# Logits by column-group products, maximum in PSUM, attention weights turned on TensorE, and a listed order

## The chip, the cores and the metric

The kernel runs on one core of a Trainium2 chip. The metric is the device time of one launch in microseconds; it is given as the median of repeated runs. One further execution was taken by the hardware profiler, and all lines quoted below come from it.

## What is computed

A conditioned transformer block for 2048 tokens of width 512 in bf16: layer norm with a shift and scale computed from a condition vector, attention with 32 heads of 16 over a dilated window of eight earlier tokens (two apart), then a second layer norm and a gated feed-forward part of width 1792.

```python
def _A_ref(x, wqkv, wo):
    H = 32; Dh = D // H; W, dil = (8, 2)
    qkv = (lambda x, *d: x.transpose(*d))((x @ wqkv).reshape(B, S, 3, H, Dh), 2, 0, 3, 1, 4)
    idx = pos[:, None] - off[None, :]          # off = arange(W) * dil
    mask = idx >= 0
    ...
    logits = jnp.einsum('bhsd,bhswd->bhsw', q, kg) * scale
    logits = jnp.where(mask[None, None, :, :], logits, -1000000000.0)
    attn = _softmax(logits, axis=-1)
    o = jnp.einsum('bhsw,bhswd->bhsd', attn, vg)
    return (lambda x, *d: x.transpose(*d))(o, 0, 2, 1, 3).reshape(B, S, D) @ wo

def _B_ref(x, w1, w3, w2):
    return jnp.einsum('bsf,fd->bsd', _silu(x @ w1) * (x @ w3), w2)
...
h = _layernorm(x, axis=-1) * (1 + ca) + sa
x = x + ga * _A_ref(h, A_wqkv, A_wo)
h = _layernorm(x, axis=-1) * (1 + cb) + sb
x = x + gb * _B_ref(h, B_w1, B_w3, B_w2)
```

## The kernel before

The 2048 tokens are 16 tiles T of 128. All of x stays on chip, as do all weights. `_build` describes the work as operations: each names its engine, what it reads and writes, a cost in ns and a key for its priority. `Program.schedule` plays the operations through a model of the engines, always taking the ready one of least priority value, and so fixes the order of every engine's queue and the buffers; `synchronize` puts in the semaphore waits; `emit` writes five straight programs, one an engine. SP issues nearly all transfers, in its own fixed order, and a transfer that waits holds up those behind it.

The stages of a tile, which overlap freely across tiles:

- LN1 (`ln_stats`): `bn_stats` (L590) and `bn_aggr` on VectorE, two small steps on POOL (L596, L598), the normalisation on VectorE (L613). `ln_T` turns the tile on TensorE (L649) and ScalarE applies scale and shift on the way out (L657).
- q, k and v (`proj_qk`, `proj_v`; L702, L721), copied out of PSUM by ScalarE; v goes to a scratch in DRAM.
- Logits (`logits`): VectorE multiplies q with the eight shifted k (L752, 4096 elements a partition). TensorE sums each head's 16 products: for each of eight window places and four column blocks, the product block is loaded as weights and a 128x32 matrix of ones, `E_sb`, streams past (L761), 32 small products a tile. Tokens lie on partitions.
- Softmax: ScalarE takes the exponential out of PSUM (L775), without a maximum. VectorE masks tile 0 (L787), adds up in three steps (L791, L793, L795), takes the reciprocal (L797) and multiplies (L798).
- AV (`values`): the weights go to a scratch in DRAM and come back in another layout (two transfers a tile, pieces of 64 bytes on the way back); v comes back from its scratch in four transfers; VectorE multiplies (L821); TensorE sums with 32 small products (L830); ScalarE copies (L836); the output projection (L843) and the residual addition on VectorE (L847) follow.
- LN2: again `bn_stats`, POOL, a bias on VectorE (L603), and the normalisation on ScalarE (L609). From FFN group 3 on (`DMA_T[1]`) the turn is a DMA transpose (six tiles), before that TensorE's.
- Feed-forward: tiles in groups (`FFN`: 2, 4, 4, 4, 2). Each group has 14 units: products with w1 and w3 (L859), SiLU on ScalarE (L865), the multiplication on VectorE (L868). Then the products with w2 (L897; L885 for the last two tiles), the output addition (L907) and the store.

Before the first loads land TensorE runs products of ones (L551, 26 times four). The condition vector is turned by a product of four rows (L519) between them.

Of the kernel before, what the change touches and what calls it, by code (L numbers as in the profile page):

```python
# [22 lines left out]
NCH = S // 512  # L23
# [5 lines left out]
LAT = {"sp": 1900, "pe": 230, "dve": 70, "act": 150, "pool": 120}  # L29
DMA_RATE = 350  # L30
TABLE_LOAD = 1300
LOOK = 250


class Pool:
    def __init__(self, name, items):
        self.name = name
        self.free = [(0, i, item, []) for i, item in enumerate(items)]
        self.n = 0

    def take(self):
        return self.free.pop(0)

    def give(self, when, slot, item, ops):
        self.n += 1
        self.free.append((when, slot, item, ops))


class Val:


    def __init__(self, name, pool=None, at=None):
        self.name = name
        self.pool = pool
        self.at = at
        self.slot = None
        self.writers = []
        self.readers = []
        self.users = []
        self.left = 0  # L60
        self.sealed = False


class Op:
    __slots__ = ("eng", "fn", "cost", "pr", "deps", "vals", "n", "start", "end", "seen", "pos", "dma", "bytes",
                 "waits", "inc", "clock", "prev", "group", "table", "key", "follow", "led", "lock")

    def __init__(self, eng, fn, cost, key):
        self.eng, self.fn, self.cost, self.key = eng, fn, cost, key
        self.pr = 0  # L70
        self.table = None
        self.follow = None
        self.led = False
        self.deps = {}
        self.vals = []
        self.prev = []
        self.end = None
        self.dma = False
        self.lock = False
        self.bytes = 0  # L80
        self.inc = None
        self.group = [self]


class Program:
# [7 lines left out]
    def op(self, eng, fn, cost, key, r=(), w=(), part=(), after=(), dma=0, table=None, lead=None, lock=None, hold=()):  # L93
        o = Op(eng, fn, cost, key)
        o.lock = eng == "pool" and not dma if lock is None else lock
        o.table = table
        if lead is not None:
            lead.follow = o
            o.led = True
# [23 lines left out]
        if dma:  # L123
            o.dma = True
            o.bytes = dma
        return o

    def dma(self, out, in_, key, nbytes, r=(), w=(), part=(), after=(), eng="sp", cost=450, group=None, transpose=False):
# [8 lines left out]
        o = self.op(eng, fn, cost, key, r=r, w=w, part=part, after=after, dma=nbytes)  # L137
# [5 lines left out]
    def schedule(self, prio):  # L143


        ops = self.ops
        users = {o: [] for o in ops}
        missing = {}
# [874 lines left out]
```

## Time and profile before

| | |
|---|---|
| median of 3 runs | 251.25 us (251.13 to 251.63) |
| span of the profiled execution | 248.6 us |
| logits, one tile on TensorE (L761) | 32 products, 0.79 us in the chain |
| AV sum, one tile (L830) | 32 products, 0.79 us in the chain |
| multiplication for logits (L752) / AV (L821) | 2280 / 2283 ns, 16 each |
| `bn_stats` (L590) / `bn_aggr` (L591) | 678 / 182 ns, 32 each |
| halving additions L791, L793, L795 (a pair) | 420, 292, 225 ns |
| ScalarE normalisation (L609) | 805 ns, 16 times |
| DMA transpose | 6, issue 1.25 us, 2.4 us to landing |
| attention weights out / back | 2.1 / 2.4 us to landing, 16 each |

The profiled execution's span runs from the first to the last instruction; the runs' times hold the launch around it as well. A matmul's recorded duration runs from its start to its modelled end and overlaps the next one; the chain of waits shows what a run of them takes end to end. PE is TensorE, PEld its weight loads, DVE VectorE, ACT ScalarE.

### The profile page before, as it was taken

To read this page: it belongs to the slowest core of one execution; us is meant where nothing else is said; L and a number is where in the kernel's file an instruction comes from. 1 tells how busy PE (TensorE), PEld (TensorE's weight loads), DVE (VectorE), ACT (ScalarE), POOL (GpSimd) and SP (SyncE) were. 2 spreads that over 40 slices of the span, in tenths; PEclk is the share of its full clock that TensorE was granted. 3 is DMA by queue.
4 is the path that set the end of the run, shared out by engine and by line. 5 is a ranking of instruction groups with operands and counts; after the bars stand their busy time and mean duration, and the time that the engine had idled before them with its cause. 6 is when DMAs were issued, how large, how long until landed. Compare 5 with 4: busy or idle time off the path is not lost.

```text
span 248.6 us, 5772 instructions
## 1 busy us (share of the span) xinstructions
PE 243.5 (98%) x2437; PEld 149.2 (60%) x2437; DVE 186.8 (75%) x289; ACT 123.3 (50%) x216; POOL 21.3 (9%) x48
## 2 busy tenths in 40 slices
PE   8989999999999999999999999999999999999995
PEld 8857665475778856545665564455544444465784
DVE  3869799999898999999899897898942344232442
ACT  2369688864783466943230577443556333110320
POOL 3223500003200110000001101000110000000000
PEclk9999999999999999999999999999999999999999
DMA  6999969679979993336779270436032000001001
GB/s 221 356 327 274 279 201 299 140 199 286 314 223 259 319 288 100 63 54 157 200 232 263 56 229 22 85 46 169 3 84 63 4 0 0 21 24 42 21 3 42
DMA packets 49393, 37.09 MB, mean 149 GB/s; under 512 B 22216, under 2 KB 40664, under 8 KB 49368
## 3 DMA queue, kind: packets, MB, share of 16 engines
q1 hardware_dynamic: 49360, 36.73, 53.3%
q8 instruction: 19, 0.31, 0.5%
q14 instruction: 6, 0.05, 0.1%
q10 hardware_dynamic: 8, 0.00, 0.0%
HBM read 30.67 MB, written 5.26 MB: 145 GB/s over the span
## 4 chain that ended last, share of the span: by engine, by line
PE 94%; DMA 4%; SPq 1%; issue 0%; DVE 0%
PE pall L859 39%; PE pall L897 17%; PE pall L702 11%; PE pall L843 6%; PE pall L721 6%; PE pall L761 5%; PE pall L830 5%; DMA sb_wqkv<-in_A_wqkv_dram 4%; PE pall L885 2%; PE pall L649 2%; SPq L135 1%; PE pall L535 0%; PE pall L565 0%; PE pall L575 0%; DVE sb_o L907 0%
## 5 line engine op out<-in xcount | busy, mean ns | idle before, releaser
L859 PE MATMUL pall<-sb_h,sb_w 128*128 128x512 bf16 (+1 forms) x560 | 101.2, 336 | 0.0
L859 PEld LDWEIGHTS pall<-sb_h,sb_w 128*128 128x128 bf16 x560 | 53.8, 98 | 41.4
L865 ACT ACTIVATE sb_sg<-pall 128x512 bf16<-128x512 f32 (+1 forms) x70 | 35.3, 511 | 64.3 <-PE pall L859 64.3
L868 DVE TENSOR_TENSOR sb_hh<-sb_sg,pall 128x512 bf16<-128x512 bf16 (+1 forms) x70 | 39.0, 575 | 28.4 <-PE pall L859 28.4
L897 PE MATMUL pall<-sb_w,sb_hh 128*128 128x512 bf16 x196 | 44.4, 379 | 0.0
L752 DVE TENSOR_TENSOR sb_pq<-sb_q,sb_kT 128x4096 bf16<-128x4096 bf16 x16 | 36.1, 2280 | 0.5 <-ACT sb_kT L711 0.5
L702 PE MATMUL pall<-sb_h,sb_wqkv 128*128 128x512 bf16 (+1 forms) x160 | 31.0, 336 | 1.4 <-DMA sb_wqkv<-in_A_wqkv_dram 1.4
L897 PEld LDWEIGHTS pall<-sb_w,sb_hh 128*128 128x128 bf16 x196 | 18.9, 98 | 21.1
L821 DVE TENSOR_TENSOR sb_vsh<-sb_vsh,sb_al 128x4096 bf16<-128x4096 bf16 x12 | 27.2, 2283 | 0.4 <-DMA sb_al<-a_scratch_dram 0.2
L590 DVE BATCH_NORM_STATS2 sb_st<-sb_x 128x6 f32<-128x512 bf16 x32 | 21.7, 678 | 4.6 <-DMA sb_x<-in_A_x_dram 4.3
L907 DVE TENSOR_TENSOR sb_o<-pall,sb_x 128x512 bf16<-128x512 f32 (+1 forms) x18 | 11.2, 629 | 17.9 <-PE pall L897 13.6
L657 ACT ACTIVATE sb_h<-pall,sb_modc 128x512 bf16<-128x512 bf16 (+1 forms) x30 | 19.2, 706 | 7.8 <-PE pall L649 7.7
L702 PEld LDWEIGHTS pall<-sb_h,sb_wqkv 128*128 128x128 bf16 x160 | 15.0, 98 | 12.9 <-issue 1.6
L596 POOL TENSOR_TENSOR sb_rs<-sb_mv,sb_cst 128x2 f32<-128x2 f32 x16 | 5.2, 326 | 159.0 <-DVE sb_mv L591 159.0
L609 ACT ACTIVATE sb_xn<-sb_x,sb_nb,sb_rs 128x512 bf16<-128x512 bf16 x16 | 12.1, 805 | 11.5 <-DVE sb_nb L603 11.5
L836 ACT ACTIVATE sb_ot<-pall 128x512 bf16<-128x512 f32 x16 | 9.5, 597 | 15.6 <-PE pall L830 13.7
L761 PEld LDWEIGHTS pall<-sb_E,sb_pq 128*128 128x128 bf16 x512 | 14.8, 96 | 2.9
L843 PE MATMUL pall<-sb_wo,sb_ot 128*128 128x512 bf16 x64 | 15.8, 378 | 0.0
L721 PE MATMUL pall<-sb_wqkv,sb_h 128*128 128x512 bf16 x64 | 15.6, 379 | 0.0
L761 PE MATMUL pall<-sb_E,sb_pq 128*128 128x32 bf16 x512 | 15.0, 176 | 0.0
L598 POOL TENSOR_TENSOR sb_rs<-sb_rs,sb_cst 128x2 f32<-128x2 f32 x16 | 13.9, 871 | 1.3
L710 ACT ACTIVATE sb_q<-pall 128x512 bf16<-128x512 f32 (+1 forms) x20 | 10.2, 517 | 6.6 <-PE pall L702 6.5
(69 smaller groups left out, 196.0 us busy)
## 6 DMA issues: line engine op xcount, KB each, us to landing
sb_vsh<-v_scratch_dram SPq DMA_DIRECT2D x48, 256.0 KB, 4.5
sb_vshx<-v_scratch_dram SPq DMA_DIRECT2D x16, 256.0 KB, 5.3
sb_w<-in_B_w_dram SPq DMA_DIRECT2D x6, 512.0 KB, 7.3
sb_w<-in_B_w_dram SPq DMA_DIRECT2D x6, 384.0 KB, 5.7
v_scratch_dram<-sb_v SPq DMA_DIRECT2D x16, 128.0 KB, 5.3
out_dram<-sb_o SPq DMA_DIRECT2D x14, 128.0 KB, 1.8
sb_wqkv<-in_A_wqkv_dram SPq DMA_DIRECT2D x3, 512.0 KB, 10.0
sb_x<-in_A_x_dram SPq DMA_DIRECT2D x3, 512.0 KB, 10.4
```

Source lines behind the costliest of these rows:

```text
L590: o = p.op("dve", lambda e, m=m, T=T: e.bn_stats(st[:, m, :], x_sb[:, T, :]), 670, ("st", m), r=[vx[T]], w=[vs])
L657: return e.activation(vh.at[:, ft, 0:n * P], b[:, j * 512:j * 512 + n * P], ACT.Identity, bias=modc[:, 8 * which + ft:8 * which + ft + 1], ...
L702: ins = e.matmul(bank(vp)[:, 0:n], wqkv[:, t, col:col + P], vh.at[:, t, 0:n], start=(t == ORDER[0]), stop=(t == ORDER[-1]))
L721: ins = e.matmul(bank(vp), vh.at[:, t, tt * P:(tt + 1) * P], wqkv[:, t, 2 * D:3 * D], start=(t == ORDER[0]), stop=(t == ORDER[-1]))
L752: return e.tensor_tensor(vp.at[:], in0, in1, ALU.mult)
L761: ins = e.matmul(b[:, c0:c0 + H], vp.at[:, w, ft, :], E_sb[:, ft, :], start=(ft == 0), stop=(ft == KT - 1))
L821: return e.tensor_tensor(v_w, v_w, a_w, ALU.mult)
L843: ins = e.matmul(bank(vy), vt.at[:, ft, :], wo[:, ft, :], start=(ft == 0), stop=(ft == KT - 1))
L859: ins = e.matmul(bank(vp)[:, 0:n], wt[:, t, fi * P:(fi + 1) * P], vh.at[:, t, 0:n], start=(t == 0), stop=(t == KT - 1))
L865: p.op("act", lambda e: e.activation(vt.at[:, 0:n], bank(vgp)[:, 0:n], ACT.Silu), c_act(n), k, r=[vgp], w=[vt], table="silu")
L868: p.op("dve", lambda e: e.tensor_tensor(vh_.at[:, 0:n], vt.at[:, 0:n], bank(vup)[:, 0:n], ALU.mult), c_dve(n), k, r=[vt, vup], w=[vh_])
L897: ins = e.matmul(bank(vz), vhh[fi].at[:, tt * P:(tt + 1) * P], w2[:, fi, :], start=(fi == 0), stop=(fi == NF - 1))
```

## The change

- **Logits.** The roles in the product are swapped: `E_sb` (32 columns) is the weight, and the product block streams past, 256 columns (8 places x 32 tokens) at a time, into one of four groups of 32 columns (`tile_position=(0, 32 * q)`): 16 products a tile. Heads now lie on partitions, 32 for each quarter of the tokens. Tile 0's mask is one more product that adds a large negative number.
- **Softmax.** VectorE takes the maximum over the window straight from PSUM and subtracts it there; the exponential is written back to PSUM; sum, reciprocal and multiplication follow on VectorE. The bank is held until then. Tiles 0 and 1 are now a pair.
- **Weights.** Two transposes a tile on TensorE (`turn`) and a copy on ScalarE replace the way through DRAM.
- **AV sums.** Tiles 8 to 15 (`AC_T`) use eight products of 512 columns in four column groups (`acc2`), ScalarE copies, and a DMA transpose turns the result. Tiles 0 to 7 keep the 32 products.
- **LN2.** The residual addition also gives the row sum; ScalarE takes the sum of squares about the mean (`ln_sums`), and POOL does four small steps for a pair. `bn_stats` and `bn_aggr` go from LN2.
- **Groups.** FFN groups of 2, 2, 4, 4, 2, 2 tiles; groups from the third on turn by DMA (12 tiles).
- **Head.** The products of ones are 26 single ones of 512 columns.
- **Order.** `schedule` and its priorities go. `place` takes `ORDER`, 1138 operation numbers, and `SLOTS`, a buffer for each value. Numbering the operations as `_build` makes them, the list reads, for what the prediction uses:
  - first loads on SP: x of tiles 0-1, the shift and scale weights, x of 2-3, wv, wq, wk, x of 4-7, a gate's weights, x of 8-11 (before: wq ahead of x 2-3 and 4-7, then wk and wv);
  - on TensorE, grouped products stand in these stretches: logits 1; 0; 3, 2; 5; 4; 8; 7; 6; 9; 11; 12; 14 with AV 8; 13, 15; AV 9 with logits 10; AV 15; 11; 10; 14; 13; 12. Tile 12's AV multiplication is the last on VectorE;
  - its end on TensorE: AV sum 12, projection 13, w2 products of tile 6 and half of tile 5, projection 12, then FFN group 3 (four tiles), groups 4 and 5 with the w2 products of tiles 8 to 13 between, and tiles 15 and 14;
  - ScalarE changes between exponential and SiLU as often as before.

```diff
-FFN = [[0, 1], [2, 3, 4, 5], [6, 7, 8, 9], [10, 11, 12, 13], [14, 15]]
-BLOCKS = [[[0]], [[1]], [[2, 3]], [[4, 5]], [[6, 7]], [[8, 9]], [[10, 11]], [[12, 13], [14, 15]]]
-VG = 2
+    return 60 + n * 137 // 128
+FFN = [[0,1],[2,3],[4,5,6,7],[8,9,10,11],[12,13],[14,15]]
+BLOCKS = [[[0, 1]], [[2, 3]], [[4, 5]], [[6, 7]], [[8, 9]], [[10, 11]], [[12, 13], [14, 15]]]
 NWARM = 18
-DMA_T = (5, 3)
+DMA_T = (5, 2)
+AC_T = 8
...
+    def place(self, order, slots):
+        for v, s in zip(self.pooled(), slots, strict=True):
+            v.slot = s
+        for o in self.ops:
+            for v in o.vals:
+                if v.pool is not None:
+                    v.at = v.pool.items[v.slot]
+                    if v.held:
+                        v.pool.last[v.slot] = v
...
+            for v in o.vals:
+                if v.pool is not None and v.pool.last.get(v.slot) is not v:
+                    before = v.pool.last.get(v.slot)
+                    if before is not None:
+                        o.prev.extend(before.users)
+                    v.pool.last[v.slot] = v
...
+    def ln_sums(Ts):
+        n, i, k = len(Ts), Ts[0], ("st", NT + Ts[-1])
+        vnm, vvs, vns = Val("nmean"), [], [Val("xn", xnpool) for T in Ts]
+        p.op("pool", lambda e: e.tensor_scalar(nm[:, i:i + n, 0], sx[:, i:i + n, 0], -1.0 / D, None, op0=ALU.mult), 250, k,
+             r=[vsx[T] for T in Ts], w=[vnm])
+        for T, vn in zip(Ts, vns):
+            vv = Val("var")
+            p.op("act", lambda e, vn=vn, T=T: e.activation(vn.at[:], x_sb[:, T, :], ACT.Square, bias=nm[:, T, :],
+                                                    accum_out=var[:, T, :]), c_act(512) + 212, ("st", NT + T), r=[vx[T], vnm],
+                 w=[vv, vn])
+            vvs.append(vv)
+        va, vr, vb = Val("vare"), Val("rstd"), Val("nbias")
+        rsn = rs[:, NT + i:NT + i + n, 0]
+        o = p.op("pool", lambda e: e.tensor_scalar(rsn, var[:, i:i + n, 0], 1.0 / D, EPS, op0=ALU.mult, op1=ALU.add), 300, k, r=vvs, w=[va])
+        o = p.op("pool", lambda e: e.tensor_tensor(rsn, rsn, bass.AP(cst, 1, [[2, P], [0, n]]), ALU.pow), 600, k, r=[va, vcst],
+                 w=[vr], lead=o)
+        p.op("pool", lambda e: e.tensor_tensor(nb[:, i:i + n, 0], nm[:, i:i + n, 0], rsn, ALU.mult), 250, k, r=[vr, vnm], w=[vb], lead=o)
+        for T, vn in zip(Ts, vns):
+            p.op("act", lambda e, vn=vn, T=T: e.activation(vn.at[:], x_sb[:, T, :], ACT.Identity, bias=nb[:, T, :],
+                                                           scale=rs[:, NT + T, :]),
+                 c_act(512) + 212, ("nm", NT + T), r=[vx[T], vr, vb], w=[vn])
...
-            def red(e, i=i, vp=vp):
-                b = bank(vl)
-                for w in range(W):
-                    for ft in range(KT):
-                        c0 = i * W * H + w * H
-                        ins = e.matmul(b[:, c0:c0 + H], vp.at[:, w, ft, :], E_sb[:, ft, :], start=(ft == 0),
-                                       stop=(ft == KT - 1))
+            def red(e, i=i, T=T, vp=vp):
+                c0 = vl.at * 512 + i * W * 32
+                if T == 0:
+                    e.matmul(PALL[0:32, c0:c0 + W * 32], ones[:, 0:32], before[:], start=True, stop=False, tile_position=(0, 0))
+                for ft in range(KT):
+                    for q in range(4):
+                        ins = e.matmul(PALL[32 * q:32 * q + 32, c0:c0 + W * 32], E_sb[:, ft, :], bass.AP(vp.at, ft * P + 32 * q, [[W * KT * P, P], [KT * P, W], [1, 2], [2, 16]]),
+                                       start=(ft == 0 and (T > 0 or q > 0)), stop=(ft == KT - 1), tile_position=(0, 32 * q))
                 return ins
-            p.op("pe", red, C_RED, ("lg", T), r=[vp, vE], part=[vl])
+            p.op("pe", red, C_RED + (110 if T == 0 else 0), ("lg", T), r=[vp, vE] + ([vbefore, vc] if T == 0 else []), part=[vl], tiled=True)
...
+    def shift(Ts, vl):
         n = len(Ts)
         k = ("sm", Ts[0])
...
-        vad, val = Val("ad"), Val("al", alpool)
-        p.dma(bass.AP(a_dram, T * P * W * H, [[W * H, 16], [16 * W * H, 8], [1, W * H]]),
-              lambda: ve.at[0][:, i].rearrange("p w h -> p (w h)"), ("ad", T), 65536, r=[va, ve], w=[vad], cost=400)
-        p.dma(lambda: val.at[:], bass.AP(a_dram, T * P * W * H, [[H, P], [16 * W * H, 8], [1, H]]), ("al", T), 65536 * 3,
-              r=[vad], w=[val], cost=400)
+        ve, vm, vs = Val("sm", smpool), Val("max"), Val("shifted")
+        o = p.op("dve", lambda e: e.tensor_reduce(ve.at[1][:, 0:n], bass.AP(PALL, bank(vl).offset, [[8 * 512, P], [W * 32, n], [1, 32], [32, W]]),
+                                                  AX.X, ALU.max), 66 + 267 * n, k, r=[vl], w=[vm], hold=[ve], lock=False)
+        def sub(e):
+            l = bank(vl)[:, 0:n * W * 32].rearrange("p (n w t) -> p n w t", n=n, w=W)
+            return e.tensor_tensor(l, l, bass.AP(ve.at[1], 0, [[64, P], [32, n], [0, W], [1, 32]]), ALU.subtract)
+        p.op("dve", sub, 74 + 267 * n, k, r=[vl, vm], w=[vs], hold=[ve, vl], lead=o, lock=False)
+        ve.shifted = vs
+        return ve
+    def exps(groups, vls, ves):
+        vxs = [Val("exp") for _ in groups]
+        def ex(e):
+            for Ts, vl in zip(groups, vls):
+                l = bank(vl)[:, 0:len(Ts) * W * 32]
+                ins = e.activation(l, l, ACT.Exp)
+            return ins
+        p.op("act", ex, sum(c_act(len(g) * W * 32) for g in groups), ("ex", groups[0][0]), r=[ve.shifted for ve in ves], w=vxs,
+             hold=ves + vls, table="exp")
+        return vxs
+    def softmax(Ts, vl, ve, vx_):
+        n = len(Ts)
+        k = ("sm", Ts[0])
+        vs, vr, va = Val("sum"), Val("rsum"), Val("attn")
+        o = p.op("dve", lambda e: e.tensor_reduce(ve.at[2][:, 0:n], bass.AP(PALL, bank(vl).offset, [[8 * 512, P], [W * 32, n], [1, 32], [32, W]]),
+                                                  AX.X, ALU.add), 66 + 267 * n, k, r=[vx_], w=[vs], hold=[ve, vl], lock=False)
+        o = p.op("dve", lambda e: e.reciprocal(ve.at[2][:, 0:n], ve.at[2][:, 0:n]), 20 + 225 * n, k, r=[vs], w=[vr], hold=[ve, vl], lead=o, lock=False)
+        p.op("dve", lambda e: e.tensor_tensor(ve.at[0][:, 0:n], bass.AP(PALL, bank(vl).offset, [[8 * 512, P], [W * 32, n], [1, 32], [32, W]]),
+                                              bass.AP(ve.at[2], 0, [[64, P], [32, n], [1, 32], [0, W]]), ALU.mult),
+             74 + 267 * n, k, r=[vr, vx_], w=[va], hold=[ve, vl], lead=o, lock=False)
+        vt, val = Val("ps_at", psum), Val("al", alpool)
+        def turn(e):
+            b = bank(vt).bitcast(bf)
+            for i in range(n):
+                at = b[:, i * 256:(i + 1) * 256].rearrange("p (q y h) -> p q y h", q=4, y=2)
+                for y in range(2):
+                    ins = e.transpose(at[:, :, y, :], bass.AP(ve.at[0], i * W * 32 + y * 16 * W, [[2 * W * 32, P], [1, P]]), ident[:])
+            return ins
+        p.op("pe", turn, 114 * n, ("at", Ts[0]), r=[va, vident], w=[vt], hold=[ve])
+        p.op("act", lambda e: e.activation(val.at[:, 0:n].rearrange("p n g h -> p (n g h)"), bank(vt).bitcast(bf)[:, 0:2 * n * P], ACT.Copy),
+             c_act(256 * n), ("at", Ts[0]), r=[vt], w=[val])
+        return val
...
+        for q in range(4):
+            p.dma(lambda q=q: vv.at[:, 2 * q:2 * q + 2, :],
+                  bass.AP(v_dram, (PAD + T * P + 32 * q) * D, [[2 * D, 16], [-DIL * D, W], [1, 2 * D]]), ("vl", T), (128, 2048),
+                  r=[vv_dram[T]] + ([vv_dram[T - 1]] if T else [vvpad]), part=[vv], group=loads, cost=640, again=True)
...
+            def acc2(e):
+                c0 = vo.at * 512
+                for y in range(2):
+                    for q in range(4):
+                        ins = e.matmul(PALL[32 * q:32 * q + 32, c0:c0 + 512], ind2[:, y, :], vv.at[:, 2 * q + y, :], start=(y == 0),
+                                       stop=(y == 1), tile_position=(0, 32 * q))
+                return ins
+            p.op("pe", acc2, C_RED, ("ac", T), r=[vv, vind2], w=[vo], tiled=True)
+            va = Val("ac", acpool)
+            p.op("act", lambda e: e.activation(va.at[:], bank(vo), ACT.Copy), c_act(512), ("ac", T), r=[vo], w=[va])
+            p.dma(lambda: vt.at[:], lambda: va.at[:], ("ot", T), (128, 1024), r=[va], w=[vt], cost=1270, transpose=True)
...
-        p.op("dve", lambda e: e.tensor_tensor(x_sb[:, T, :], bank(vy), x_sb[:, T, :], ALU.add), c_dve(512), ("rs", T), r=[vy],
-             w=[vx[T]])
+        p.op("dve", lambda e: e.scalar_tensor_tensor(x_sb[:, T, :], bank(vy), 1.0, x_sb[:, T, :], op0=ALU.mult, op1=ALU.add,
+                                                     accum_out=sx[:, T, :]), c_dve(512) + 12, ("rs", T), r=[vy], w=[vx[T], vsx[T]])
```

397 lines of the change are left out of this document (134 added, 263 removed), and 93 rows, old and new, of tables (ORDER, SLOTS, vhh).

## The prediction

> **What bounds the kernel now.** I read the summary and the 40 slices first.
>
> ```profile
> PE 243.5 (98%) x2437; PEld 149.2 (60%) x2437; DVE 186.8 (75%) x289; ACT 123.3 (50%) x216; POOL 21.3 (9%) x48
> PE   8989999999999999999999999999999999999995
> DVE  3869799999898999999899897898942344232442
> PEclk9999999999999999999999999999999999999999
> ```
>
> TensorE has no gap after the second slice, at full clock; VectorE is almost as full until slice 29 and then has room. The chain of waits gives the real spacing of products (start to start), which the mean durations hide.
>
> ```profile
> 3.44 9.98 DMA sb_wqkv<-in_A_wqkv_dram
> 13.55 1.03 PE pall L702 x8
> ...
> 20.24 0.89 PE pall L649 x16
> ...
> 81.22 0.79 PE pall L761 x32
> 82.02 0.79 PE pall L830 x32
> ...
> 239.91 6.13 PE pall L885 x56
> ```
>
> From 13.55 to 246.04 us it is TensorE alone; before that it waits for wk, and the last addition and store take 2.6 us. So the end moves one for one with TensorE's work, while VectorE keeps up. Spacings: 512 columns 0.216 us (7 in 1.51), 256 columns 0.109 (6.13/56), a transpose 0.056 (0.89/16), and 0.0246 for the 32 small products of a logits or AV tile (0.79).
>
> ```profile
> 0.00:20.00 20.00, 17.44 (x210) 14.91 (x211) 13.09 (x40) 9.39 (x21) 5.75 (x24) 1.00 0.97 296
> 20.00:175.60 155.60, 155.60 (x1794) 94.05 (x1792) 145.09 (x198) 90.92 (x154) 13.77 (x20) 1.00 0.70 188
> ```
>
> The windows (length, then PE, PEld, DVE, ACT, POOL) up to the end of the last AV multiplication at 175.6 us: VectorE worked 158.2 us and idled 17.4, 6.9 of them in the first 20 us. It had 10.5 us of slack afterwards, and TensorE never waited for it.
>
> **The change on TensorE.** The sum is against the profiled 248.6 us; the median of the runs, 251.25, lies 2.65 higher, which I add at the end.
>
> 1. Logits: 16 tiles of 32 small products at 0.79 us become 16 products of 256 columns in four column groups. No row shows groups side by side. Four at once: four rounds of 0.109, 0.44 us; one after another 16 x 0.109 = 1.74. I take 0.46, side by side with one issue step of 0.025, as each group writes other partitions: 16 x 0.33 = 5.3 us saved; the other end loses 15.2.
> 2. AV sums of tiles 8 to 15: 0.79 becomes 8 products of 512 columns, 2 x 0.216 + 0.025 = 0.46 side by side, 1.73 in series. 8 x 0.33 = 2.6 saved, or 7.5 lost.
> 3. Switching. In the listed order the 24 grouped tiles stand in 20 stretches (T3/T2, T14 with AV 8, T13/T15 and AV 9 with T10 are adjacent). The nearest row is the one product of another shape between full ones, in the timeline:
>
> ```profile
> 6.00 0.28 PE L551 MATMUL pall<-sb_ones 128*128 128x128 bf16 x2
> 6.21 0.17 PE L519 MATMUL pall<-sb_ident,sb_c4s 4*128 4x4 bf16 x1
> 6.32 0.40 PE L551 MATMUL pall<-sb_ones 128*128 128x128 bf16 x4
> ```
>
> The second ones product starts at 6.06, the small one 0.15 later (0.056 is usual), the next 0.11 later (0.025 is usual): 0.18 us for the visit. 20 x 0.18 = 3.6 us. Ends: nothing, and the full depth (379 ns recorded less 216 spacing, 0.163) on both sides, 6.5.
> The Trainium skill, TensorEngine Tiling (Array Packing), Tiling Modes, says that changing the mode drains the array; this speaks against the change. The visit above agrees in kind, with 0.09 us a side; by a whole depth a side the sum would be 2.9 us worse.
> 4. New transposes of the weights: 32 x 0.056 = 1.8 us. LN2 groups from the third on go by DMA, 12 tiles instead of 6: 24 transposes fewer, -1.3. Their DMAs land in 2.4 us each.
> 5. Fourteen 512-wide FFN units become 28 of 256 (1.735 us against 2 x 0.87) and one mask product for tile 0: +0.2.
> 6. Head. Bytes ahead of wk are the same (3.0 MB), so it lands at 13.4 again. With wv sent ahead of wq and wk, TensorE can do two V tiles (1.73), six q products (0.65) and 16 transposes (0.9) before that, 3.3 us, where it did 13 q products and 8 transposes, 1.9: -1.4. Price: x4-7 comes 1 MB later (about 15 us, as the 3.5th MB was wv before, and V products start at 15.47), so LN1 of tiles 4 to 7 ends at some 18.5 to 21; 5.9 us of q and k work from 13.4 on covers it. Without that cover up to 2 us go.
>
> Sum: -5.3 - 2.6 + 3.6 + 1.8 - 1.3 + 0.2 - 1.4 = -5.0.
>
> **The change on VectorE.** This decides whether TensorE can use it.
>
> ```profile
> L798 DVE TENSOR_TENSOR sb_attn<-sb_ex,sb_ssum 128x512 bf16<-128x512 f32 x7 | 4.8, 692 | 0.2
> L907 DVE TENSOR_TENSOR sb_o<-pall,sb_x 128x512 bf16<-128x512 f32 x14 | 9.5, 688 | 13.6 <-PE pall L897 13.6
> L797 DVE RECIPROCAL sb_ssum<-sb_ssum 128x64 f32<-128x64 f32 x7 | 3.9, 552 | 0.2
> L731 ACT ACTIVATE sb_v<-pall 128x512 bf16<-128x512 f32 x16 | 9.5, 602 | 3.7 <-PE pall L721 3.3 <-DMA v_scratch_dram<-sb_v 0.4
> ```
>
> Softmax before: 7 pairs of 2.18 us, two singles of 1.48, the mask 0.43: 18.7. After: 8 pairs of maximum, subtraction, sum, product (0.69 each: PSUM and SBUF sources cost alike at 512 elements) and the 0.55 reciprocal: 3.31, 26.5 us. A reduction or a write into PSUM has no row; the strided PSUM read on ScalarE (602 ns) costs as much as a straight one (599), so I take 0.69 for each; below by the halving adds (420 ns), above double. Removed before the last AV: 13 LN2 statistics of 0.79 (bn_stats start to next start) = 10.3, their biases 1.0. In the listed order less stands ahead of the last AV (tile 12's): 42 FFN products, most of 256 columns (2.2 less), two output additions fewer (1.3), one residual addition fewer (0.6). With the small copies for ind2: 158.2 + 7.8 - 10.3 - 1.0 - 2.2 - 1.3 - 0.6 + 0.1 = 150.7 us.
>
> Behind tile 12's AV, TensorE has, in the list: its sum and switch 0.64, two output projections 1.7, one and a half w2 tiles 4.5, FFN group 3 (24.3), groups 4 and 5 (24.4), six w2 tiles 18.1, the last two 6.1: 79.9 us. So TensorE, ending at 246.0 - 5.0 = 241.0, wants that AV at 161.1. VectorE, with 6.9 us idle in the head, can have it at 157.6. Slack is 3.5 us against 10.5, so some waits now reach TensorE: I take 1.0, between 0 and 7 (VectorE idling 17.4 again ends at 168.1).
>
> **Costed at nothing.** ScalarE gains 16 squares of 0.8 (the row of L609), 8 turns of 0.6 and short units, some 20 us on 123 of 248, hidden by its idle half; table loads stay at eight by the order. Tiles 8 to 15 now wait for ScalarE's copy (0.6) and a transpose (2.4 to land) between AV sum and output projection; TensorE's queue behind the projection holds FFN and w2 products, and the list puts at least 5.4 us of others between the two, so it costs nothing unless SP is late. SP sends 14 more transposes of 1.25 us issue (17.5) and loses 32 attention transfers, about 14; a transpose waiting at its head holds the V loads behind it, and so the AV multiplication, which is part of the 0 to 7 above. POOL's four steps instead of two a pair delay LN2 by about 1 us, covered by the FFN group in front. The attention transfers (16,384 pieces of 64 B and 2,048 of 512 B) go, which takes load off the transfers between 20 and 100 us, where no wait on them exceeds 0.2.
>
> Span 248.6 - 5.0 + 1.0 = 244.6, time 247.3.
>
> **Rivals.**
> A. Switching is nearly free and VectorE keeps up: 244.6 - 3.6 - 1.0 = 240.0, time 242.7. For: the small visit is another shape (4 rows); against: its 0.15 and 0.11.
> B. VectorE becomes the bound, slower. It idles as long as before, 17.4 us up to tile 12's AV: 168.1 + 0.2 + 79.9 + 2.6 = 250.8, time 253.4. It decides from 8 us of idle after the first 20, where the end meets 251.25; before had 10.5. For: each pair's chain now runs matmul, maximum, ScalarE, sum, transpose, ScalarE, AV, and holds its PSUM bank throughout; reductions above 0.69 come on top. Against: much of that idle was VectorE waiting for TensorE (3.5 us at L868 alone), which now comes sooner.
> C. Weight loads are not hidden in column groups. By the spacing row a round is then four issues of 0.0246 ahead of the product: logits 4 x (0.098 + 0.109) = 0.83, sums 2 x (0.098 + 0.216) = 0.63: 16 x 0.37 + 8 x 0.17 = 7.3 worse, time 254.6. For: the loads run 149 us and were hidden only in full-array form; against: L761's 32 loads of 128 columns fit in 0.79.
> The Trainium skill, same page, Restrictions and Gotchas, states that column tiling excludes the fast weight load; nothing here shows it.
> D. Groups run one after another, so the change doesn't do what it says: 15.2 + 5.3 and 7.5 + 2.6 worse, 30.6: 277.9.
>
> **Chances.** Forecast 0.45 (its own range 245 to 250), A 0.20, B 0.21, C 0.10, D 0.04. Range 241 to 254.6: it takes in most of A, B and reaches C's point; some 0.16 lie outside (D, half of C, the part below 241). A measurement here tells apart about 0.2%, 0.5 us. Faster: the forecast, A, and none of B: 0.64 after leaving 0.01 to the edge; same 0.06 (the nearer part of B); slower 0.30.
>
> **What would show it.** Step 1 and 2: a logits tile in the chain at about 0.46 us, its products four to a start; 0.8 is C, 1.7 is D. Step 3: 0.1 us gaps at each stretch's ends. VectorE: reductions near 0.69, last AV at 162 us. If TensorE idles over 5 us between 20 and 165 while VectorE is full, B. If the head has TensorE idle around 19 to 22, step 6 fell. The forecast is wrong if the sum of TensorE's spacings falls by less than 3 us or more than 9.

## The result, and the profile after

The changed kernel takes 248.58 us (median of 9 runs, 247.22 to 250.37) against 251.17 us (9 runs, 250.22 to 251.63): a ratio of 0.9894, with 95% interval 0.9869 to 0.9919, so 2.6 us or 1.1% faster. The profiled execution has a span of 246.3 us where it was 248.6. Its own time was 248.09, 1.8 more than the span, as in every run of this kernel. Two runs below, 252.96 us with the old sums and 251.08 with more v buffers alone, lie over 1.5% above the fastest of their kernel and are left out of the ratios.

The summary and two rows of the 40 slices of the changed kernel:

```profile
PE 238.7 (97%) x2003; PEld 141.9 (58%) x2032; DVE 179.4 (73%) x276; ACT 137.6 (56%) x273; POOL 23.1 (9%) x66
PE   7999999999999999999999999999989999999995
DVE  4588999999999999999999998844233612452442
```

VectorE's room starts at slice 27 instead of 30, as its last AV multiplication now ends at 162.7 us instead of 175.6. TensorE shows its first slice under 9 in the middle of the kernel (the 30th, about 181 us). The weight loads number 2032 and the recorded products 2003; 29 product records are missing, and the holes they leave are not waits.

The chain of waits of the changed kernel (start, length, what):

```profile
10.60 0.65 PE pall L661 x3
...
13.86 5.89 PE pall L642 x54
...
24.28 0.55 PE pall L702 x16
...
67.49 0.79 PE pall L788 x32
...
108.33 3.60 DMA sb_vshx<-v_scratch_dram
111.95 2.30 DVE sb_vshx L777
114.25 0.14 issue
114.39 0.61 PE pall L805 x8
...
163.07 0.55 PE pall L805 x8
...
176.06 0.69 DVE sb_hh L842
176.74 0.61 DVE sb_o L881
...
177.38 3.68 DMA out_dram<-sb_o
...
181.08 0.70 DVE sb_o L881
```

A grouped tile, logits (L702) or AV sum (L805), stands at 0.55 us where the old one, L788, still takes 0.79. V products (L661) now run at 10.6 us, before wk has landed. New are two kinds of pieces outside TensorE, and it waits for both: a load of v with VectorE's multiplication behind it (L777, at 108.33), and an output store with VectorE's addition (L881, at 177.38).

How a grouped tile takes its time can be read from TensorE's timeline around the last AV sum (start, busy time, line, number of instructions):

```profile
161.82 1.24 PE L871 MATMUL pall<-sb_w,sb_hh 128*128 128x512 bf16 x5
163.00 0.62 PE L805 MATMUL pall<-sb_vshx,sb_ind 128*32 128x512 bf16 x8
163.54 1.04 PE L817 MATMUL pall<-sb_wo,sb_ot 128*128 128x512 bf16 x4
```

The groups of the same tile show each product's duration (partitions x elements, count, then busy us and mean ns):

```profile
L805 PE MATMUL pall<-sb_vshx,sb_ind 128*32 128x512 bf16 x24 | 1.8, 384 | 0.2 <-DVE sb_vshx L777 0.2
L805 PEld LDWEIGHTS pall<-sb_vshx,sb_ind 128*32 128x32 bf16 x24 | 0.4, 94 | 1.3 <-issue 0.5 <-DVE sb_hh L842 0.4 <-DVE sb_vshx L777 0.4
```

Eight products of 384 ns end within 0.62 us: two rounds of four, 0.227 apart, and 384 ns for the last. In the records the four of a round start within 10 ns of each other. Taking each start against the usual spacing, the first grouped product comes 0.093 us late and so does the first full one after the tile: 0.19 us for a visit. Between them a logits tile takes 0.46 us (0.556 to the next full product, less 0.093) and an AV sum 0.46 (0.549 less 0.093).

VectorE's new work, from the groups:

```profile
L714 DVE TENSOR_REDUCE sb_mx<-pall 128x64 f32<-128x512 f32 x8 | 5.5, 682 | 0.0
L719 DVE TENSOR_TENSOR pall<-pall,sb_mx 128x512 f32<-128x512 f32 x8 | 5.6, 699 | 0.3
L744 DVE TENSOR_REDUCE sb_ssum<-pall 128x64 f32<-128x512 f32 x8 | 5.4, 678 | 0.0
L747 DVE TENSOR_TENSOR sb_attn<-pall,sb_ssum 128x512 bf16<-128x512 f32 x8 | 5.5, 691 | 0.3
```

Reduction, subtraction in place and multiplication all cost 0.68 to 0.70 us, so reading with a stride and writing back to PSUM cost nothing more than other work on 512 elements. The windows up to the end of the last AV multiplication (length, then PE, PEld, DVE, ACT, POOL; then clock, DMA share and GB/s):

```profile
0.00:20.00 20.00, 18.42 (x155) 11.78 (x157) 12.56 (x39) 9.24 (x23) 6.88 (x26) 1.00 0.96 310
20.00:162.70 142.70, 140.35 (x1348) 80.77 (x1366) 137.18 (x175) 98.13 (x185) 13.59 (x32) 1.00 0.74 196
```

VectorE worked 12.56 + 137.18 = 149.7 us up to that point and idled 7.4 in the head and 5.5 after it.

TensorE's last product starts 2.4 us earlier (243.38, before 245.76). Its spacings from start to start, summed by kind of work, say where that comes from:

| TensorE, us | predicted | in the traces |
|---|---|---|
| logits (tile 0's mask with them) and AV sums, with their switches | -4.3 (-5.3 - 2.6 + 3.6) | -4.3 (25.7 to 21.4) |
| turns, LN2 transposes, FFN split | +0.7 | +0.7 |
| head: work done before 13.5 us | -1.4 | -1.25 (8 V products and 5 transposes more, 7 q products fewer) |
| waits after the head | +1.0 | +2.15 (none before) |
| the rest | 0 | +0.3 (0.2 of it a product of ones at 20.9) |
| sum | -4.0 | -2.4 |

The second and third rows are the traces' counts of products times the usual spacings, and about 0.1 us is left over. The waits are one of 0.79 us at 181 us, one of 0.41 at 114.4, one of 0.29 at 155.4 and five of 0.10 to 0.18. The second is easily missed, as TensorE's recorded work runs on almost up to it:

```profile
113.52 0.62 PE L702 MATMUL pall<-sb_pq,sb_E 128*32 128x256 bf16 x16
114.39 0.61 PE L805 MATMUL pall<-sb_vshx,sb_ind 128*32 128x512 bf16 x8 [0.25 <-DVE sb_vshx L777]
```

The tile's last product starts at 113.87 and another could follow 0.11 later; the sum starts at 114.39, after VectorE's multiplication, which ends at 114.25.

### The profile page after: what moved, and what is told of

The parts are those of the page before. It is cut to its first block, busy times and chain, and to the rows that moved or that the text cites. A ratio compares the mean times of both kernels' runs of the same rounds, so it can differ in the third digit from the quotient of the medians.

```text
span 246.3 us, 4944 instructions
## 1 busy us (share of the span) xinstructions
PE 238.7 (97%) x2003; PEld 141.9 (58%) x2032; DVE 179.4 (73%) x276; ACT 137.6 (56%) x273; POOL 23.1 (9%) x66
## 4 chain that ended last, share of the span: by engine, by line
PE 87%; DMA 5%; DVE 3%; issue 1%; ACT 1%; SPq 1%
PE pall L833 34%; PE pall L871 16%; PE pall L642 11%; PE pall L661 6%; PE pall L817 5%; PE pall L480 3%; PE pall L702 3%; PE pall L788 3%; PE pall L859 2%; DMA sb_vsh<-v_scratch_dram 2%; PE pall L589 2%; DMA out_dram<-sb_o 1%; DMA sb_vshx<-v_scratch_dram 1%; PE pall L805 1%; DVE sb_vshx L777 1%
## 5 line engine op out<-in xcount | busy, mean ns | idle before, releaser
L833 PE MATMUL pall<-sb_h,sb_w 128*128 128x256 bf16 (+1 forms) x666 | 102.5, 307 | 1.2 <-DVE sb_o L881 0.6
L833 PEld LDWEIGHTS pall<-sb_h,sb_w 128*128 128x128 bf16 x672 | 64.5, 98 | 35.4 <-DVE sb_o L881 1.3
L839 ACT ACTIVATE sb_sg<-pall 128x256 bf16<-128x256 f32 (+1 forms) x84 | 35.1, 453 | 54.7 <-PE pall L833 41.1
L842 DVE TENSOR_TENSOR sb_hh<-sb_sg,pall 128x256 bf16<-128x256 bf16 (+1 forms) x84 | 39.5, 503 | 26.7 <-PE pall L833 20.4
L777 DVE TENSOR_TENSOR sb_vsh<-sb_vsh,sb_al 128x4096 bf16<-128x4096 bf16 x12 | 27.2, 2283 | 1.1 <-DMA sb_vsh<-v_scratch_dram 1.1
L881 DVE TENSOR_TENSOR sb_o<-pall,sb_x 128x512 bf16<-128x512 f32 (+1 forms) x18 | 11.1, 627 | 23.1 <-PE pall L871 13.4
L597 ACT ACTIVATE sb_h<-pall,sb_modc 128x256 bf16<-128x256 bf16 (+1 forms) x26 | 15.4, 663 | 9.6 <-PE pall L589 9.5
L661 PE MATMUL pall<-sb_wqkv,sb_h 128*128 128x512 bf16 x58 | 15.4, 380 | 0.4 <-issue 0.2
L517 DVE BATCH_NORM_STATS2 sb_st<-sb_x 128x6 f32<-128x512 bf16 x16 | 10.8, 675 | 2.7 <-DMA sb_x<-in_A_x_dram 2.7
L821 DVE SCALAR_TENSOR_TENSOR sb_x<-pall,sb_x 128x512 bf16<-128x512 f32 x16 | 10.7, 684 | 2.1 <-PE pall L817 2.1
L543 ACT ACTIVATE sb_xn<-sb_x,sb_nm 128x512 bf16<-128x512 bf16 x16 | 11.4, 719 | 1.3 <-POOL sb_nm L539 1.3
L811 ACT ACTIVATE sb_ac<-pall 128x512 bf16<-128x512 f32 x8 | 4.8, 598 | 12.0 <-PE pall L805 12.0
L574 ACT ACTIVATE sb_h<-sb_h,sb_modc 128x512 bf16<-128x512 bf16 (+1 forms) x16 | 10.2, 697 | 2.2 <-DMA sb_h<-sb_xn 2.2
```

The costliest lines, as they stand in the source:

```text
L543: p.op("act", lambda e, vn=vn, T=T: e.activation(vn.at[:], x_sb[:, T, :], ACT.Square, bias=nm[:, T, :], accum_out=var[:, T, :]), c_act(512 ...
L597: return e.activation(vh.at[:, ft, 0:n * P], b[:, j * 512:j * 512 + n * P], ACT.Identity, bias=modc[:, 8 * which + ft:8 * which + ft + 1], ...
L661: ins = e.matmul(bank(vp), vh.at[:, t, tt * P:(tt + 1) * P], wqkv[:, t, 2 * D:3 * D], start=(t == ORDER[0]), stop=(t == ORDER[-1]))
L777: return e.tensor_tensor(v_w, v_w, a_w, ALU.mult)
L833: ins = e.matmul(bank(vp)[:, 0:n], wt[:, t, fi * P:(fi + 1) * P], vh.at[:, t, 0:n], start=(t == 0), stop=(t == KT - 1))
L839: p.op("act", lambda e: e.activation(vt.at[:, 0:n], bank(vgp)[:, 0:n], ACT.Silu), c_act(n), k, r=[vgp], w=[vt], table="silu")
```

## The experiments

Each kernel is the changed one with the edit shown. The runs came in three batches; the kernel before ran beside each, at 251.29, 251.18 and 251.27 us. A ratio is to that kernel, with its 95% interval; "the changed kernel" is the 248.58 us above.

**Logits products twice.** Does TensorE's work still set the end?

```diff
+                for _ in range(2):
                     for ft in range(KT):
                         for q in range(4):
```

> The changed kernel with each tile's sixteen grouped logits products issued twice (the second pass starts the sums anew). Theory T (TensorE sets the end, VectorE only comes near): a tile takes 0.44 us more, 16 x 0.436 = 7.0 us, so about 255.5 us, ratio to the kernel before 1.017 (0.989 for the changed kernel). Rival V (VectorE sets the end through the attention part): TensorE has room there, so less than 2 us more, 250.5 or below, ratio under 0.998. If the groups do not run side by side a pass costs 1.7 us and the time rises by some 28.

Measured: 254.02 us, ratio 1.0117 (1.0088 to 1.0146), span 252.6: +5.4 by the medians, +6.3 by the spans. VectorE has the same work, so an end that VectorE set would hardly move. The groups count 512 products, and where there is a wait it is VectorE's for TensorE:

```profile
L703 PE MATMUL pall<-sb_pq,sb_E 128*32 128x256 bf16 x512 | 16.8, 271 | 0.0
L715 DVE TENSOR_REDUCE sb_mx<-pall 128x64 f32<-128x512 f32 x8 | 5.5, 685 | 1.2 <-PE pall L703 1.2
```

16 more passes at 0.44 are 7.0 us; 77 to 90% of that reaches the end. Most of what is missing by the spans is the wait at 181 us, which this trace does not have (the store in front of it landed in 1.9 us). TensorE sets the end.

**One more visit to the groups in every logits tile.** What does a switch cost?

```diff
+                e.matmul(PALL[0:32, c0:c0 + 16], ones[:, 0:32], ones[:, 0:16], start=True, stop=True, tile_position=(0, 0))
+                e.matmul(PALL[:, c0:c0 + 16], ones[:, 0:P], ones[:, 0:16], start=True, stop=True)
```

> The changed kernel with one more visit to column groups ahead of every logits tile: a grouped product of 16 columns, then a full one of 16 columns, both overwritten by the tile's own sums. The two products alone are 16 x 0.05 = 0.8 us. T with a switch cost of 0.18 us a visit, as I read it from the small product among the ones before: 16 x 0.23 = 3.7 us more, about 252.3, ratio 1.004. T with free switches: 0.8 us more, 249.4, ratio 0.992. T with a whole depth of 0.163 on each side: 16 x 0.38 = 6.0, 254.6, ratio 1.013. Rival V: below 1 us in any case.

Measured: 250.71 us (249.5 to 252.97), ratio 0.9984 (0.9957 to 1.001), +2.1 by the medians; the profiled span of 250.7 holds a wait of 1.5 us at 61.7 that the changed kernel's does not. The time alone, with its scatter, leaves the price between nothing and 0.18. TensorE's timeline of one tile is clearer:

```profile
24.42 0.18 PE L698 MATMUL pall<-sb_ones 128*32 128x16 bf16 x1
24.53 0.18 PE L699 MATMUL pall<-sb_ones 128*128 128x16 bf16 x1
24.64 0.62 PE L704 MATMUL pall<-sb_pq,sb_E 128*32 128x256 bf16 x16
25.20 1.04 PE L661 MATMUL pall<-sb_wqkv,sb_h 128*128 128x512 bf16 x3
```

Each change of shape puts 0.11 us between starts that otherwise lie 0.025 apart: 0.09 us a side and 0.18 for a visit, as the prediction read it from the small turn of the condition vector. The Trainium skill, TensorEngine Tiling (Array Packing), Tiling Modes, states that changing the mode drains the array; these rows agree in kind and put the price at 0.09 us a side, not a whole depth.

**Without the maximum.** Is VectorE's load behind the waits? This kernel leaves out the maximum and its subtraction, with two tiny memsets in their places.

```diff
-        o = p.op("dve", lambda e: e.tensor_reduce(ve.at[1][:, 0:n], ..., AX.X, ALU.max), ...
+        o = p.op("dve", lambda e: e.memset(ve.at[1][:, 0:1, 0:2], 0.0), ...
-            return e.tensor_tensor(l, l, bass.AP(ve.at[1], ...), ALU.subtract)
+            return e.memset(ve.at[1][:, 0:1, 2:4], 0.0)
```

> The changed kernel without the maximum and the subtraction (two small memsets stand in their places), which takes 8 x 1.3 = 10 us from VectorE and none from TensorE. T: only what VectorE's lateness costs TensorE goes, 0.5 to 2 us: 246.5 to 248, ratio 0.981 to 0.988, and the runs scatter less. V: most of the 10 us, under 243.5, ratio under 0.970.

Measured: 248.55 us (248.04 to 249.78), ratio 0.9908 (0.988 to 0.9936), span 246.2. VectorE worked 171.2 us, 8.2 less, and nothing came of it in the time; I had expected half a microsecond to two. TensorE's waits of this kernel (total, times, longest):

```profile
PE pall L831 <- DVE sb_o L879: 0.9, 1, 0.9
PE pall L831 <- ACT sb_h L597: 0.3, 1, 0.3
PE pall L589 <- ACT sb_xn L554: 0.3, 1, 0.3
```

The largest, behind the output addition, is the changed kernel's wait at 181 us; it is still there, 1.0 us by the spacings instead of 0.8, so it does not come from VectorE's load. Two others partly do: the wait at 114 us fell from 0.41 to 0.16 and that at 155 from 0.29 to 0.14. But two of 0.23 behind ScalarE came up at 50 and 53 us, and TensorE waits 2.2 us in all in both kernels.

**The maximum twice.** How much room has VectorE left?

```diff
+            for at in (2, 1):
+                ins = e.tensor_reduce(ve.at[at][:, 0:n], ..., AX.X, ALU.max)
```

> The changed kernel with a second reduction of each pair's logits into a buffer that the sum later overwrites: VectorE gets 8 x 0.6 = 4.8 us more. T with a slack of 3.5 us for VectorE: 0.5 to 2.5 us more, 249 to 251, ratio 0.991 to 1.000. V: 4.8 us more, 253.4, ratio 1.009.

Measured: 251.68 us (249.31 to 252.95), ratio 1.0015 (0.9989 to 1.0042): +3.1 by the medians, +4.2 by the spans (250.5 against 246.3), for 4.5 us more on VectorE (183.9 against 179.4), and more than the 0.5 to 2.5 expected. TensorE now waits in many places:

```profile
PE pall L838 <- DVE sb_o L886: 1.1, 2, 0.9
PE pall L838 <- DVE sb_hh L847: 0.8, 1, 0.8
PE pall L589 <- DVE sb_attn L752: 0.4, 1, 0.4
PE pall L793 <- DVE sb_vsh L782: 0.4, 2, 0.2
```

Less work gains nothing, more work costs most of itself: VectorE is not the bound of the changed kernel, but stands close behind it, by 0.3 us (4.5 less 4.2) to 1.4 (4.5 less 3.1), and the medians scatter by more than that. The slack of 3.5 us in the prediction did not absorb the added work.

**AV sums of tiles 8 to 15 as before.** Do the grouped sums pay, with the DMA transposes they bring?

```diff
-AC_T = 8
+AC_T = 16
```

The eight transposes' places are taken out of the order; nothing else moves.

> The changed kernel with the AV sums of tiles 8 to 15 done as in tiles 0 to 7 (32 small products, ScalarE's copy straight into the projection's operand); the eight DMA transposes go, the order of all else stays. By the changed kernel's trace a grouped sum takes 0.59 us and 0.1 on the way in, 0.69, against 0.79: T expects 8 x 0.1 = 0.8 us more, 249.4, ratio 0.993. Rival W (the way through ScalarE and the DMA transpose holds TensorE up): 0.5 to 1.5 us less, ratio 0.984 to 0.987.

Measured: 250.18 us (248.59 to 252.96), ratio 0.9951 (0.9918 to 0.9984): +1.6, span 248.6 with waits of 0.9 at 59.9 and 0.75 at 171.9. From rows, the old sums cost 8 x 0.79 = 6.3; the grouped ones cost 8 x 0.46 = 3.7, and six visits of 0.19 (two sums share theirs with a logits tile), 1.1. So 1.5 was due. The rival, that the transposes on SP cost more than the sums save, fell.

**Four output buffers instead of two.** What is the wait at 181 us? TensorE, VectorE and SP in the changed kernel's timeline:

```profile
177.38 0.34 SPq L124 DMA_DIRECT2D out_dram<-sb_o  x1
178.15 3.56 SPq L124 DMA_TRANSPOSE sb_h<-sb_xn  x2
...
181.08 0.69 DVE L881 TENSOR_TENSOR sb_o<-pall,sb_x 128x512 bf16<-128x512 f32 x1 [3.73 <-DMA out_dram<-sb_o]
...
181.83 0.39 PE L833 MATMUL pall<-sb_h,sb_w 128*128 128x512 bf16 x1 [0.63 <-DVE sb_o L881]
```

The output addition waits 3.73 us until a store that was issued at 177.38 has landed and its buffer is free; the median store lands in 1.8. Two transposes follow it in the queue. The addition holds a PSUM bank, and TensorE's next FFN product wants that bank. There are two buffers, but by the list only one is in turn here: the result added at 167.64 sits in the other until 194.54, when SP sends its store behind two other stores and four transposes, so the additions at 169.15, 176.74 and 181.08 all share one.

```diff
-    osb = [nc.alloc_sbuf_tensor_at(f"sb_o{i}", ...) for i in range(2)]
+    osb = [nc.alloc_sbuf_tensor_at(f"sb_o{i}", ...) for i in range(4)]
...
+            slots[at] = 100 + i % 4
```

The second part of the edit hands the four out in turn, so it also undoes the sharing.

> The changed kernel with four output buffers in turn in place of two. In its trace VectorE waits 3.7 us at 177.4 us for a store to free a buffer, and TensorE then 0.8 us at 180.8 for the bank that VectorE was to empty. T: 0.5 to 1.0 us less, 247.6 to 248.1, ratio 0.985 to 0.987, and no gap there. Rival: another wait takes its place (VectorE's next, or the transposes ahead of the store), no difference.

Measured: 247.81 us (247.28 to 248.65), ratio 0.9867 (0.9826 to 0.9909), span 246.1, -0.8 against the changed kernel. The timeline of the same place:

```profile
175.68 8.58 PE L836 MATMUL pall<-sb_h,sb_w 128*128 128x512 bf16 x39
...
177.35 1.28 DVE L884 TENSOR_TENSOR sb_o<-pall,sb_x 128x512 bf16<-128x512 f32 x2
```

The two additions follow each other at once, and TensorE runs 39 products without a gap. The wait is gone in the trace; the 0.8 us of the medians fits it, though the intervals overlap. The two profiled spans differ by only 0.2: here the head is 0.3 us later and other waits are longer (0.44 at 155 us, 0.36 at 40). More buffers and another order of the buffers were not tried apart, nor the two buffers with the stores sent in another order.

The store itself can be compared over all traces, as the changed kernel and its variants each have it with the first transpose 0.77 us behind. In nine of the thirteen it lands after 3.3 to 4.1 us, in four (logits twice, more visits, old sums, shorter ones) after 1.7 to 1.9. So transposes behind it do not by themselves make it late. In the late ones 120 of its 128 packets are through 1.35 us after the issue; the last eight begin to come 1.0 us after that or later, and the very last is through at 2.8 to 3.6. In eight of these nine a 16 KB load of instructions starts 0.9 to 1.2 us after the issue, while the packets still move; in the four prompt ones none starts before 1.4. That is what goes together in the traces; no run sets the two apart. The wait follows in the five late traces with two output buffers (0.6 to 1.1 us) and in none of the four late ones with four.

**Shorter products of ones.** The turn of the condition vector starts at 7.56 us where it was 6.21 before, because 16 products of ones of 512 columns now stand ahead of it.

```diff
-            return e.matmul(bank(vw), ones[:, 0:P], ones[:], start=True, stop=True)
+            n = 336 if i < 18 and i not in (7, 10) else 512
+            return e.matmul(bank(vw)[:, 0:n], ones[:, 0:P], ones[:, 0:n], start=True, stop=True)
```

> The changed kernel with the 16 products of ones ahead of the condition vector's turn cut from 512 to 336 columns, so that they end at about 6.1 us and not 7.5; everything up to the first V product waits for that turn (7.56 us against 6.21 in the kernel before). T: the first V product starts up to 1.3 us earlier, and TensorE has that much more work done when wk lands: 0.6 to 1.3 us less, 247.3 to 248.0, ratio 0.984 to 0.987. Rival: the shift and scale weights or wv land no earlier than they are used now, so nothing, 248.6.

Measured: 248.13 us (247.16 to 249.79), ratio 0.9872 (0.9826 to 0.9918), -0.45, not told apart from the changed kernel. The profiled execution has a span of 248.0. TensorE's waits, and one place:

```profile
PE pall L834 <- ACT sb_v L672: 1.5, 1, 1.5
...
PE pall L449 <- DVE sb_c4s L447: 0.8, 1, 0.8
```

```profile
61.65 0.60 ACT L672 ACTIVATE sb_v<-pall 128x512 bf16<-128x512 f32 x1 [2.14 <-DMA v_scratch_dram<-sb_v]
...
62.30 1.36 PE L834 MATMUL pall<-sb_h,sb_w 128*128 128x256 bf16 x9 [1.51 <-ACT sb_v L672]
```

The turn now waits 0.8 us for VectorE and starts at 6.13, and the first logits tile starts at 23.57 us instead of 24.21, so 0.6 us of the head is gained. It is lost again at 61 us, where ScalarE waits for a store of v to free one of three buffers, and TensorE for the bank that ScalarE has not emptied. The same place held 1.5 us in the run with more visits, 0.9 in the one with the old sums and 0.5 in the one with the maximum twice, and nothing in the changed kernel's profile.

**Both of these**, four outputs and shorter ones:

> Four output buffers and the shorter ones together. If both act and are separate: 1.1 to 2.3 us less, 246.3 to 247.5, ratio 0.980 to 0.985. If one of them only moves a wait: the gain of the other alone.

Measured: 247.57 us (246.59 to 247.9), ratio 0.985 (0.981 to 0.9891), span 245.8: 1.0 less than the changed kernel, and 0.24 less than with four outputs alone, which is within the scatter. The granted clock of the first 20 us was 0.91 here, 1.00 in the changed kernel.

**Products of one group after another.** Must the order of issue alternate the groups?

```diff
-                for ft in range(KT):
-                    for q in range(4):
+                for q in range(4):
+                    for ft in range(KT):
```

> The changed kernel with the sixteen logits products of a tile issued group by group (four of one column group, then the next), the same products otherwise. T: products run side by side only while neighbours in the queue belong to different groups, so a pass costs up to 4 x 0.436 = 1.74 us and not 0.44, and 16 x 1.3 = 21 us are added: 265 to 270, a tile at 1.7 to 1.85 us. Rival: the queue lets later groups pass, then nothing changes, 248.6.

Measured: 248.5 us (two runs, 248.21 and 248.8), ratio 0.9885 (0.9828 to 0.9943), span 247.0; the expected loss of some 21 us did not come. The chain:

```profile
24.60 0.58 PE pall L702 x16
```

A tile takes 0.58 us instead of 0.55, and its products still start in rounds of four (0, 13, 27, 40 ns, then 123 and on). In the changed kernel the four start at 0, 4, 7 and 10 ns; 13 is about four times such a step, as the first product of each group now stands behind four of the group before. The records do not name a product's group, but in series 16 products would need 1.74 us. So a product of a later group starts while earlier ones of another group wait. The Trainium skill, TensorE: Matmul & The Clock Gate, Part 3: Packing small matmuls — row/col tiling, states that products start strictly in the order of the program; this trace speaks against it for column groups.

**More v buffers.** Is the wait at 61 us what scatters the runs? Six buffers for v instead of three, handed out in turn, alone, with four outputs, and with four outputs and the shorter ones:

```diff
-    vb = [sb([P, D], bf, f"v{i}") for i in range(3)]
+    vb = [sb([P, D], bf, f"v{i}") for i in range(6)]
```

> Six v buffers alone, two output buffers. Theory: the gap at 60 us goes from every run and the one at 181 us stays: median 248.0 (247.5 to 248.4), scatter about half of the changed kernel's 3.2 us. Rival: the scatter comes from elsewhere (the loads of v, the start), median 248.6 and the same scatter.

> Four output buffers, and six buffers in turn for the copies of v on their way to the scratch in place of three. In four of the eight traces so far TensorE loses 0.9 to 1.7 us at 60 us, where ScalarE waits for a v store that sits behind the weight loads. If that gap and the one at 181 us are what makes the runs of the changed kernel scatter: median 247.2 (246.8 to 247.6), ratio 0.984, and no run above 248.5. If the wait only moves to the next v copy: 247.8 like the four output buffers alone.

> Four output buffers, six v buffers and the shorter products of ones. If the three gains are separate (0.8, 0.4 and 0.4 us): 246.9, ratio 0.983. If the short ones only move the wait (in their trace the turn then waited for VectorE, and the span was no shorter): 247.2, like the first two.

| buffers | median, us (range, 6 runs) | ratio | span |
|---|---|---|---|
| v alone | 247.85 (246.65 to 251.08) | 0.9859 (0.9816 to 0.9903) | 245.8 |
| v and outputs | 247.77 (246.03 to 249.09) | 0.9857 (0.9807 to 0.9906) | 245.2 |
| v, outputs, short ones | 247.75 (246.45 to 249.22) | 0.9854 (0.9814 to 0.9895) | 247.4 |

None of the three traces has the wait at 60 us, and yet the scatter stayed (2.7 us for v alone even without its longest run, 3.1 and 2.8 for the others), so the theory that the v buffers make it fell. All three, and the two kernels with four outputs above, lie between 247.6 and 247.9; they cannot be ranked. They beat the kernel before clearly, and the changed one by some 0.8 us with overlapping intervals.

## Why the prediction was right, and where it was off

The prediction was 247.3 us; 248.58 came, faster as forecast. Of the 1.3 us, the span is 1.7 longer than the 244.6 forecast. Against that, 2.3 us instead of 2.65 lie between the profiled span and the median. In the runs of the changed kernel the time is 1.8 above the span, in those of the kernel before 1.9 to 2.0, so the rest of that figure only says where the profiled execution lies among its runs. Of the gain of 4.0 us, 2.6 came.

- **Bound.** Right. Twice the logits products lengthen the kernel by 5.4 us; VectorE 8.2 us shorter does not shorten it. The last sign of being wrong, a fall of TensorE's spacings by less than 3 us, does not say whether waits count: without them, as the -5.0 was added up, they fall by some 4.5, with them by 2.4.
- **Steps 1 and 2.** Groups side by side was right: rounds 0.109 and 0.227 apart, tiles of 0.46, against rivals D (1.74 a tile) and C (0.83). The runs say nothing of how the loads are hidden, only that they cost nothing here: 94 ns each, 512 of them in the doubled kernel, and the tile is still four rounds and a switch.
- **Step 3.** Right: 0.19 a visit against 0.18, about 20 of them, and so rival A fell. With tiles of 0.46 as taken, steps 1 to 3 save the 4.3 us worked out.
- **Steps 4 and 5.** Right by count. The switches and the turns give back 3.8 and 1.8 of the 7.9 us that steps 1 and 2 save, and that is why so large a cut in the small products moves the time so little.
- **Step 6.** -1.25 against -1.4. V products do run before wk lands. The later condition turn may take some of it back: with shorter products of ones ahead of it the first logits tile starts 0.6 us earlier.
- **VectorE.** Its work was right: 149.7 us of work against 150.7 up to tile 12's AV, 0.68 to 0.70 an instruction against 0.69, and 80.4 us of TensorE behind its sum against 79.9 (whose terms add up to 79.7); the 80.4 hold the wait of 0.8. The AV ended at 162.7, between the earliest 157.6 and rival B's 168.1; VectorE idled 5.5 us after the head, and B decides from 8. The slack of 3.5 us was too much: the maximum twice, 4.5 us more, cost 3.1 to 4.2.
- **The waits.** This is the term that was mis-sized: 1.0 taken, 2.15 measured, within its 0 to 7. I gave them to VectorE's smaller slack and to transposes holding back V loads at SP's head. For two of them, 0.7 us, that fits: the AV multiplications in front of the sums at 114.4 and 155.4 start 0.28 and 0.76 us late behind a load of v, and with less work on VectorE these waits shrink. The largest, 0.8 us, is of a kind that the prediction did not have: an output buffer that is freed by a store that lands late, while the list keeps the other buffer full; four buffers in turn remove it in the trace. Transposes on SP were costed as issue time, and why the store takes 3.7 us instead of 1.8 is not shown. The five others (0.10 to 0.18) were not tried one by one.
- **Two readings of the kernel before.** TensorE's gap before wk lands is in the third slice, not the second, and ScalarE waited 0.4 us between 20 and 100 us for a store of v, so "no wait on them exceeds 0.2" was not so. It is the kind of wait that grew to 1.5 us at 61 us in the kernel with shorter ones.

Open: why the runs scatter. The changed kernel's lie 3.2 us apart, those of the kernel before in the same comparison 1.4; but in the three batches of experiments the kernel before spreads over 2.5 to 3.7 us itself (23, 17 and 11 runs). A wait at some 60 us that comes and goes was the candidate, and more v buffers removed it from the traces and did not narrow the runs. Seven executions on record had a mean granted clock of 0.992 to 0.993 instead of 1.00, and five of them are the longest runs of their kernel (of the kernel before, the two longest), so a lower clock goes with the longest ones; what lowers it is not shown. Open too is why the store at 177 us lands late in some executions.

## What to carry to other kernels

Price column groups by rounds plus 0.19 us for each visit: here a 0.79 us tile came to about 0.65, and one that follows another grouped tile directly to 0.46. When an engine's work is cut on a path that had no gaps, look next at every buffer that used to come free just in time, and at the order in which stores free the buffers; and test the load of the second engine in both directions: less work that gains nothing and more work that costs nearly all of itself is an engine that stands close behind.

## What the runs showed of the hardware

- Products of four column groups start within 10 ns of each other, and the order in which the groups are issued hardly matters (0.58 against 0.55 us a tile).
- A reduction out of PSUM over a strided window and a subtraction written back into PSUM cost as much as plain work of that size (682 and 699 ns for 512 elements).
- A row sum taken along with an operation is not free: reading it is an instruction of its own, 82 ns on VectorE and 196 ns on ScalarE. The groups of the changed kernel:

```profile
L821 DVE DVE_READ_ACCUMULATOR sb_x<-pall,sb_x 128x1 f32 x16 | 1.3, 82 | 0.0
L543 ACT ACTIVATION_READ_ACCUMULATOR sb_xn<-sb_x,sb_nm 128x1 f32 x16 | 3.1, 196 | 0.0
```

- A 128 KB store landed after 1.7 to 1.9 us in four traces and after 3.3 to 4.1 in nine. In eight of the nine a 16 KB load of instructions starts 0.9 to 1.2 us after the store's issue, and the store's last eight packets of 128 come 1.0 us or more behind the others; no run isolates it.
- The granted clock of the first 20 us was 0.91 in two of fourteen traces (four outputs with shorter ones, and all three edits) and 1.00 in the others, one of them with the shorter ones alone. Whether the shorter ones have a part in it is not shown.
